# Routing attention and a bilinear FFN on one core: the second head pair's q and k loaded and transposed among the first pair's steps, and the first values ahead of the second scores

## The chip, the core and the metric

One core of a Trainium2 chip runs one program. Its engines are TensorE (PE; its weight loads are listed as PEld), VectorE (DVE), ScalarE (ACT), GpSimd (POOL) and SyncE (SP), which here issues most DMAs. The metric is the device time of one execution in microseconds. The kernel before took 1065.71 us as the median of four runs (1064.76, 1065.71, 1065.71 and 1065.93).

## The reference

Four batches of eight heads, 768 positions, head dimension 64. Every q and k row is assigned to the most similar of 16 centroids of its head; a query attends only to keys with its own assignment. The result, as 3072 tokens of 512 values, goes through a bilinear FFN of inner width 1536.

```python
q_assign = np.argmax(np.einsum('bhsd,hcd->bhsc', q_n, c_n), axis=-1)
k_assign = np.argmax(np.einsum('bhsd,hcd->bhsc', k_n, c_n), axis=-1)
mask = q_assign[:, :, :, None] == k_assign[:, :, None, :]
scores = scale * np.matmul(q, k.transpose(0, 1, 3, 2))
scores = np.where(mask, scores, -1000000000.0)
...
attn = attn / (np.sum(attn, axis=-1, keepdims=True) + 1e-09)
return np.matmul(attn, v).astype(np.float32)
...
a = x @ w_a
b = x @ w_b
return (a * b @ w_out).astype(np.float32)
```

## The kernel before, in words

The work goes by pairs of heads: 16 pairs p (4 batches of 4). A pair has 12 units: 2 halves of its 768 queries times 6 blocks of 128 keys. A unit's scores for both heads are one PSUM tile of 128 keys x 2 x 384 queries. Two units make a group g; a pair is six groups, so the main loop has 96 steps and three more to finish. The order of all instructions on each engine is the order in which the program issues them: nothing is rescheduled.

For each pair, q and k are loaded with positions on the partitions (`load`, L193 to L210, one DMA for each of q, k and head, 192 KB in pieces of 256 B, issued by SP) and transposed by PE, twelve blocks of 128 x 128 in three PSUM tiles (`prep_transpose(p, i)`, L335 to L350, one copy out of PSUM for each i). From these come the similarities to the centroids (`prep_sim`, L358, and its copy L366), turned back by PE (`prep_across`, L372), five DVE operations that make one-hot assignments (`prep_assign`, L405 to L409), and PE transposes of these (L418; for the first pair `prep_onehot_first`, L434, with a copy on ACT, L438, and one on DVE, L441).

`score` (L539) adds two products in PSUM, one of the one-hots (scaled by 2**60, bf16) and one of q and k, so that pairs of different assignment fall far below the others; then ACT takes the exponential (L548) into a tile `pt`, of which there are four. `weigh` multiplies these by v (L580). `add_up` (L569, DVE, later POOL too) sums the exponentials over the key blocks into `acc`, and `denominators` (L603) sums `acc` over the partitions by a product with ones. Only three PSUM tiles named m and two for scores (s) exist; one more (O) collects the values.

Pools set when things may start. The tile `qk` for loaded q and k exists once. The first pair takes another way in (`load_first`, L212 to L221): two DMAs bring its q (on SP's queue) and k (on ACT's) into a tile `h`, a buffer meant for the FFN's inner values, of which there are two, and DVE and ACT reorder them into `qk` (L224). `load(1)` then waits for the first pair's transposes, since it needs `qk` again.

The start is written out by hand before the loop: `keep_busy(n)` (L328) issues n transposes of the identity into a PSUM tile that nobody reads, while PE waits for other engines. In the loop, step g issues the scores of group g, the additions and the values of group g - 1, one of six preparation steps for the next pair (`prep_steps`), the rounding of the FFN weights as they fall due (`round_w`, L275 to L297: four DVE operations, one on ACT, one on POOL, then one more on DVE), and FFN pieces as far as credit goes. For the second pair, preparation step 0 issues `prep_transpose(1, 0)` and `(1, 1)`; the last third, `(1, 2)`, and `load(2)` follow at the end of the same step.

Of the kernel before, what the change touches and what calls it, by code (L numbers as in the profile page):

```python
# [8 lines left out]
FP32 = mybir.dt.float32  # L9
# [21 lines left out]
P = 128  # L31
# [105 lines left out]
def short_path(nc, tc, ctx, c, cn, centroids_in, casts, n_far, q, k, v,  # L137
# [3 lines left out]
    B, H, S, D = q.shape  # L141
    NC = 16
    DM, DF = moe_w_a.shape
    NJ = S // P
# [6 lines left out]
    def pool(name, bufs, space=None):  # L151
        kw = {} if space is None else {"space": space}
        return ctx.enter_context(tc.tile_pool(name=name, bufs=bufs, **kw))

    zero = pool("zero", 1)
    qkp = pool("qkp", 1)
# [8 lines left out]
    hp_ = pool("hp", 2)  # L165
# [9 lines left out]
    ident, identb, ones, rank = c["ident"], c["identb"], c["ones"], c["rank"]  # L175
# [10 lines left out]
    def by_blocks(p):  # L186
        return p >= HP

    def load(p):
        if p >= NPAIR:  # L190
            return
        b, hp = divmod(p, HP)
        if by_blocks(p):  # L193
            t = qkp.tile([P, 2, S // 32, 32], FP32, name="qk")
            for w, src in enumerate((q, k)):
                for n in range(4):
                    a, d = divmod(n, 2)
                    nc.sync.dma_start(
                        out=t[32 * n:32 * n + 32, w],
                        in_=src[b, 2 * hp + a, :, 32 * d:32 * d + 32].rearrange(  # L200
                            "(j t) d -> t j d", t=32))
            qks[p] = t
            return
        t = qkp.tile([P, 2, NJ, 2, D], FP32, name="qk")
        for w, src in enumerate((q, k)):
            for a in range(2):
                nc.sync.dma_start(
                    out=t[:, w, :, a, :],
                    in_=src[b, 2 * hp + a].rearrange("(p j) d -> p j d", j=NJ))
        qks[p] = t  # L210

    def load_first():  # L212

        t = qkp.tile([P, 2, NJ, 2, D], FP32, name="qk")
        rows = hp_.tile([P, 2, 2, NJ * D], FP32, name="h")
        for eng, w, src in ((nc.sync, 0, q), (nc.scalar, 1, k)):
            eng.dma_start(out=rows[:, w], in_=src[0, 0:2].rearrange(
                "a (p j) d -> p a (j d)", j=NJ))
        qks[0] = t
        return t, rows  # L220
# [20 lines left out]
            in_=v[b, 2 * hp:2 * hp + 2].rearrange("a (p j) d -> p a (j d)", j=NJ))  # L241

    first = load_first()
    centroids_in()
    order_first(*first, 0, nc.vector.tensor_copy)
    order_first(*first, 1, nc.scalar.copy)
# [76 lines left out]
    idle = ps_o.tile([P, 512], FP32, name="O")  # L323

    def keep_busy(n):

        for _ in range(n):
            nc.tensor.transpose(out=idle[:, 0:P], in_=ident, identity=ident)  # L328
# [7 lines left out]
    def prep_transpose(p, i):  # L336
        if i == 0:
            qkTs[p] = qtp.tile([P, 2 * S], FP32, name="qkT")
        ps = ps_m.tile([P, 512], FP32, name="m")
        for n in range(4):  # L340
            w, j = divmod(4 * i + n, NJ)
            nc.tensor.transpose(  # L342
                out=ps[:, n * P:(n + 1) * P],
                in_=qks[p][:, w, j].rearrange("p a d -> p (a d)"),
                identity=ident)
        dst = qkTs[p][:, i * 512:(i + 1) * 512]
        if p == 0 and i != 1:
            nc.vector.tensor_copy(out=dst, in_=ps)
        else:
            nc.scalar.copy(out=dst, in_=ps)  # L350
# [77 lines left out]
    def prep_onehot_first(kq):  # L428

        ohTs[0] = ohT_bufs[0]  # L430
        ps = ps_m.tile([P, 1024], BF16, name="m")
        for n in (3, 4, 5, 0, 1, 2):
            w, t = divmod(n, 3)
            nc.tensor.transpose(out=ps[:, n * P:(n + 1) * P],  # L434
                                in_=oh_all[:, 4 * t + 2 * w + kq, :],
                                identity=identb)
        c0 = kq * HB
        nc.scalar.activation(out=ohTs[0][:, S + c0:S + c0 + HB],  # L438
                             in_=ps[:, HB:S], func=AF.Identity, scale=FAR,
                             bias=nfar[:, 0:1])  # L440
        nc.vector.tensor_copy(out=ohTs[0][:, c0:c0 + HB], in_=ps[:, 0:HB])  # L441
# [55 lines left out]
    def prep_steps(p):  # L497
        if p >= NPAIR:
            return [lambda: None] * 6

        def both(*fs):
            return lambda: [f() for f in fs]

        if by_blocks(p):
            steps = prep_by_blocks(p)
            ready = [lambda s=s: todo.extend(s) for s in steps]
            ready[1] = both(lambda: prep_sim(p), lambda: load_v(p), ready[1])
            return ready

        return [  # L510
            both(lambda: prep_transpose(p, 0), lambda: prep_transpose(p, 1)),
            both(lambda: prep_sim(p), lambda: load_v(p)),
            lambda: todo.extend(prep_assign(prep_across(p))),
            lambda: None,
            lambda: prep_onehot(p, 1),
            lambda: None,
        ]
# [56 lines left out]
    def weigh(us):  # L574
        for u in us:
            p, hf, j = where(u)
            if j == 0:
                O_of[0] = ps_o.tile([P, 512], FP32, name="O")
            for a in range(2):
                nc.tensor.matmul(out=O_of[0][a * D:(a + 1) * D, 0:HB],  # L580
                                 lhsT=vs[p][:, a, j, :], rhs=probs[u][:, a, :],
                                 start=(j == 0), stop=(j == NJ - 1))
        if j < NJ - 1:
            return
        b, hp = divmod(p, HP)
        if hp == 0 and hf == 0:
            while b > 1 and len(ffn) > FREE_XT:
                ffn.popleft()[1]()
            xTs[b] = xtp.tile([P, NCH, S], FP32, name="xT")
        nc.scalar.copy(out=xTs[b][:, hp, hf * HB:(hf + 1) * HB],  # L590
                       in_=O_of[0][:, 0:HB])
# [403 lines left out]
    NG = NPAIR * GPP  # L995
# [13 lines left out]
    for i in range(8, len(w_parts)):  # L1009
        due.setdefault(23 + int((i - 8) / 1.5), []).append(i)  # L1010

    keep_busy(18)
    prep_transpose(0, 0)
    centroids_across()
    prep_transpose(0, 1)
    prep_transpose(0, 2)
    casts()
    for r, factor in ((slice(0, P // 2), 1.0), (slice(P // 2, P), FAR)):
        nc.vector.tensor_scalar(out=rank_far[r], in0=rank[r], scalar1=factor,
                                scalar2=None, op0=ALU.mult)  # L1020
    load(1)
    load_v(0)
    load_w(0)
    load_w(1)
# [3 lines left out]

    across = prep_across(0)
    rest_of_first = score((0, 1))  # L1030
    keep_busy(4)
    for kq in range(2):
        for step in prep_assign(across, kq):
            step()
        prep_onehot_first(kq)
        if kq == 0:
            keep_busy(5)
            rest_of_first()
            keep_busy(7)
    for g in range(NG + 3):  # L1040
        p, l = divmod(g, GPP)
        if l == 0:
            ready = prep_steps(p + 1)
        now = (2 * g, 2 * g + 1)
        before = (2 * g - 2, 2 * g - 1)
        if 0 < g < NG:
            score(now)
        check_inverses()
        if 0 < g <= NG:
            for u in before:  # L1050
                add_up(u)
        flush_w()
        if 0 < g <= NG:
            weigh(before)
        if g < NG:
            ready[l]()
        late = int(g > EARLY)
        if g % 3 == late and 0 < g - late:
            denominators(*divmod(g // 3 - 1, 2))
        parts = due.get(g, [])  # L1060

        def round_next():
            if parts:
                i = parts.pop(0)
                round_w(i)
                load_w(i + 2)

        round_next()
        if g <= EARLY:
            first, second = 4, 1  # L1070
        else:
            first, second = 5, 3 if g < NG else 2
        ph = {first: (p, 0), second: (p - 1, 1)}.get(l)
        halved = ph in den_of
        if halved:
            todo.extend(normalize(*ph))
        if ffn:
            credit += PER_GROUP[(g > 2 * BG + 3) + (g > 3 * BG + 3)]
            least = FREE_ROOM if halved and ph[1] and (ph[0] + 1) % HP == 0 else 0
            while len(ffn) > least and credit > 0:  # L1080
                cost, piece = ffn.popleft()
                credit -= cost
                piece()
                if todo:
                    todo.popleft()()
                round_next()
        else:
            credit = 0
        round_next()
        while todo:  # L1090
            todo.popleft()()
        if halved:
            ffn_ready(*ph)
        if l == 0 and p + 1 < NPAIR:
            if not by_blocks(p + 1):
                prep_transpose(p + 1, 2)
            load(p + 2)
        if l == 4 and p + 1 < NPAIR and not by_blocks(p + 1):
            prep_onehot(p + 1, 0)

    def some_ffn(n):
        for _ in range(n):
# [17 lines left out]
                     start=True, stop=True)  # L1120
# [227 lines left out]
```

## Time and profile before

| what | value |
|---|---|
| median of four runs | 1065.71 us |
| time of the profiled execution | 1064.65 us |
| its span | 1062.9 us, 13065 instructions |
| granted TensorE clock, mean | 0.999 |
| DVE, ACT, POOL busy | 67%, 24%, 33% of the span |
| DMA | 46.18 MB, 43 GB/s on average |
| q of the first pair, issue to landing | 3.9 us |
| k of the first pair, issue to landing | 4.4 us |

The span is measured inside the profiled execution, whose time is 1.75 us longer. The profile lists the busy time of each engine, groups of instructions by source line, the chain of work that ended last, and the instructions in order of time. A line of that last view gives start and duration in microseconds, the engine, the source line, the operation with what it writes and reads, and a count where equal instructions follow one another; in brackets stands the time that the engine had been idle and whose end it waited for. The ends of matmuls are modelled, so the starts are the better guide.

### The profile page before, as it was taken

The page shows a single profiled execution, that of the slowest core. Times are in us where ns is not written, and L with a number is a line of the kernel's source. Part 1 is how long each engine was busy: PE and PEld are TensorE (multiplying, and loading weights), DVE is VectorE, ACT ScalarE, POOL GpSimd, SP SyncE. Part 2 cuts the span into 40 slices and gives each one's busy share as a digit, 9 for nine tenths or more (in the row PEclk, how much of TensorE's full clock was granted, in tenths as well). Part 3 has the DMA queues.
Part 4 walks back from the last instruction along what each step waited for, and adds up shares of the span by engine and source line. Part 5 has one row for each costly group of instructions (what it writes and reads, how often), then busy time and mean ns, then how long its engine had stood idle before and what let it go on. Part 6 is the DMA issues. An engine that isn't in the chain of part 4 may idle for free.

```text
span 1062.9 us, 13065 instructions
## 1 busy us (share of the span) xinstructions
PE 1049.5 (99%) x4756; PEld 605.5 (57%) x4756; DVE 708.0 (67%) x1402; ACT 260.0 (24%) x501; POOL 354.3 (33%) x329
## 2 busy tenths in 40 slices
PE   8999999999999999999999999999999999999997
PEld 5444455554556665455445766555545687555686
DVE  5778877887857447676757736767565846676762
ACT  5665333233322221212222121122122200000000
POOL 1111345454533323443545422444334310222200
PEclk9999999999999999999999999999999999999999
DMA  5334243525130120202020030300000000000001
GB/s 169 94 72 99 84 105 104 124 74 134 62 47 16 41 43 20 39 4 45 4 45 1 25 65 24 46 0 20 0 4 1 11 30 21 0 1 1 0 31 33
DMA packets 120504, 46.18 MB, mean 43 GB/s; under 512 B 106608, under 2 KB 115824, under 8 KB 120432
## 3 DMA queue, kind: packets, MB, share of 16 engines
q1 hardware_dynamic: 120016, 44.85, 18.3%
q8 instruction: 39, 0.64, 0.2%
q10 hardware_dynamic: 416, 0.43, 0.1%
q14 instruction: 33, 0.27, 0.1%
HBM read 37.78 MB, written 6.29 MB: 41 GB/s over the span
## 4 chain that ended last, share of the span: by engine, by line
PE 92%; DVE 5%; issue 1%; POOL 1%; DMA 0%; ACT 0%; DVEq 0%; POOLq 0%
PE m L767 30%; PE m L893 20%; PE s L539 14%; PE O L580 12%; PE m L663 11%; PE m L603 2%; PE m L358 1%; DVE raw L723 1%; PE m L342 0%; DVE raw L750 0%; DVE acc L569 0%; DVE xT L723 0%; POOL xT L635 0%; DVE ha L777 0%; DMA wo_sb<-in_centroids_dram 0%
## 5 line engine op out<-in xcount | busy, mean ns | idle before, releaser
L548 ACT ACTIVATE pt<-s 128x768 f32<-128x768 f32 x192 | 145.4, 808 | 307.4 <-PE s L539 253.8
L569 POOL TENSOR_TENSOR acc<-acc,pt 128x384 f32<-128x384 f32 x144 | 151.9, 1068 | 59.8 <-ACT pt L548 43.6
L782 POOL TENSOR_TENSOR h<-h,ha 128x384 f32<-128x384 f32 x72 | 72.6, 1016 | 235.9 <-DVE ha L777 234.4
L580 PE MATMUL O<-pt,v 128*64 128x384 f32 x768 | 145.1, 499 | 0.0
L539 PE MATMUL s<-qkT 64*128 64x384 f32 x768 | 139.6, 482 | 0.0
L777 DVE TENSOR_TENSOR ha<-ha,m 128x384 f32<-128x384 f32 x126 | 66.9, 546 | 74.1 <-PE m L767 73.3
L777 DVE TENSOR_TENSOR h<-h,m 128x384 f32<-128x384 f32 x126 | 67.3, 549 | 64.3 <-PE m L767 63.5
L569 DVE TENSOR_TENSOR acc<-acc,pt 128x384 f32<-128x384 f32 x96 | 73.7, 793 | 35.9 <-POOL acc L569 35.0
L580 PEld LDWEIGHTS O<-pt,v 128*64 128x64 f32 x768 | 46.6, 136 | 86.4 <-issue 84.8
L539 PEld LDWEIGHTS s<-qkT 64*128 64x128 f32 x768 | 70.5, 187 | 31.4 <-issue 0.2
L893 PE MATMUL m<-wo_sb,h 128*128 128x256 f32 x384 | 87.5, 382 | 0.0
L635 POOL TENSOR_TENSOR xT<-xT,acc 128x384 f32<-128x384 f32 x32 | 32.9, 1029 | 147.9 <-DVE acc L630 121.3
L893 PEld LDWEIGHTS m<-wo_sb,h 128*128 128x128 f32 x384 | 72.1, 190 | 16.0 <-issue 4.2
L767 PE MATMUL m<-raw 128*128 128x384 f32 x192 | 70.4, 489 | 0.9 <-DVE ha L777 0.9
L663 PE MATMUL m<-xT,wa_sb 128*128 128x384 f32 x192 | 67.4, 493 | 0.7 <-POOL xT L635 0.7
L663 PE MATMUL m<-xT,wb_sb 128*128 128x384 f32 x192 | 66.8, 491 | 0.0
L893 PE MATMUL m<-xT,h 128*128 128x256 f32 x288 | 65.4, 382 | 0.1
L893 PEld LDWEIGHTS m<-xT,h 128*128 128x128 f32 x288 | 54.1, 190 | 11.7 <-issue 1.7
L767 PE MATMUL m<-xT,wa_sb 128*128 128x384 f32 x144 | 52.9, 491 | 0.4 <-DVE rest L899 0.4
L767 PE MATMUL m<-xT,wb_sb 128*128 128x384 f32 x144 | 52.9, 490 | 0.0
L767 PE MATMUL m<-xT,size 128*128 128x384 f32 x144 | 52.9, 490 | 0.0
L663 PEld LDWEIGHTS m<-xT,wa_sb 128*128 128x128 f32 x192 | 35.4, 190 | 30.5 <-ACT pt L548 3.6
(164 smaller groups left out, 1444.6 us busy)
## 6 DMA issues: line engine op xcount, KB each, us to landing
raw<-in_moe_w_a_dram SPq DMA_DIRECT2D x12, 512.0 KB, 4.3
raw<-in_moe_w_b_dram SPq DMA_DIRECT2D x12, 512.0 KB, 3.5
raw<-in_moe_w_out_dram SPq DMA_DIRECT2D x12, 512.0 KB, 3.2
qk<-in_q_dram SPq DMA_DIRECT2D x48, 96.0 KB, 2.9
qk<-in_k_dram SPq DMA_DIRECT2D x48, 96.0 KB, 3.6
v<-in_v_dram SPq DMA_DIRECT2D x24, 192.0 KB, 3.9
out_dram<-rest SPq DMA_DIRECT2D x24, 128.0 KB, 1.7
v<-in_v_dram SPq DMA_DIRECT2D x4, 384.0 KB, 4.6
```

The costliest lines, as they stand in the source:

```text
L358: nc.tensor.matmul(out=ps[32 * kq:32 * kq + 32, 0:HB], lhsT=cTb[:, hp, :], rhs=qkTs[p][:, kq * HB:(kq + 1) * HB], start=True, stop=True)
L539: nc.tensor.matmul(out=s[:, a, 0:HB], lhsT=Ts[p][r, S + j * P:S + (j + 1) * P], rhs=Ts[p][r, hf * HB:(hf + 1) * HB], start=start, stop=not ...
L548: nc.scalar.activation(out=pt, in_=s[:, :, 0:HB], func=AF.Exp, scale=SCALE)
L569: eng.tensor_tensor(out=acc[:, a, :], in0=probs[u - 1][:, a, :] if j == 1 else acc[:, a, :], in1=probs[u][:, a, :], op=ALU.add)
L580: nc.tensor.matmul(out=O_of[0][a * D:(a + 1) * D, 0:HB], lhsT=vs[p][:, a, j, :], rhs=probs[u][:, a, :], start=(j == 0), stop=(j == NJ - 1))
L603: nc.tensor.matmul(out=ps[a * D:(a + 1) * D, 0:HB], lhsT=ones, rhs=t[:, a, :], start=(n == 0), stop=(n == len(terms) - 1))
L635: nc.gpsimd.tensor_tensor(out=x, in0=x, in1=den, op=ALU.mult)
L663: nc.tensor.matmul(out=ps[:, 0:HB], lhsT=w_sb[:, ch, f * P:(f + 1) * P], rhs=xTs[b][:, ch, t0:t0 + HB], start=(ch == 0), stop=(ch == NCH - 1))
L767: nc.tensor.matmul(out=ps[:, 0:HB], lhsT=A[l][c], rhs=rhs[c], start=(c == 0), stop=(c == 1))
L777: nc.vector.tensor_tensor(out=out, in0=in0, in1=ps, op=op)
L782: nc.gpsimd.tensor_tensor(out=to, in0=to, in1=box[name], op=ALU.mult)
L893: nc.tensor.matmul(out=ps[:, 0:HN], lhsT=A[l][f // 3][:, f % 3, :], rhs=B[r][f // 2][:, f % 2, :], start=(f == 0), stop=(f == N2 - 1))
```

## The change

`load(1)` no longer uses `qk` but the second `h` tile, and moves to the very start, right behind the loads of the first pair; so its four DMAs come second on SP's queue, and the loads of v, of the first weights and of the third pair no longer stand behind them. The second pair's three `prep_transpose` calls leave loop step 0: the first takes the place of three fillers after the first scores, the other two that of the seven fillers after the first pair's one-hot product, in front of the second half of its one-hot transposes. The third copy out of PSUM goes to DVE instead of ACT. The first 18 fillers become twelve products of the tile `ones` (64 x 64) and 16 fillers. In loop step 1 the values of group 0 are issued ahead of the scores of group 1; in all later steps the order is as before.

```diff
-        t = qkp.tile([P, 2, NJ, 2, D], FP32, name="qk")
+
+        own, name = (hp_, "h") if p == 1 else (qkp, "qk")
+        t = own.tile([P, 2, NJ, 2, D], FP32, name=name)
...
     first = load_first()
+    load(1)
     centroids_in()
...
-        if p == 0 and i != 1:
+        if p == 0 and i != 1 or p == 1 and i == 2:
             nc.vector.tensor_copy(out=dst, in_=ps)
...
-            both(lambda: prep_transpose(p, 0), lambda: prep_transpose(p, 1)),
+            lambda: p > 1 and (prep_transpose(p, 0), prep_transpose(p, 1)),
...
-    keep_busy(18)
+    for _ in range(12):
+        nc.tensor.matmul(out=idle[0:D, 0:D], lhsT=ones, rhs=ones, start=True,
+                         stop=True)
+    keep_busy(16)
     prep_transpose(0, 0)
...
-    load(1)
     load_v(0)
...
     rest_of_first = score((0, 1))
-    keep_busy(4)
+    prep_transpose(1, 0)
+    keep_busy(1)
     for kq in range(2):
         for step in prep_assign(across, kq):
             step()
+        if kq == 1:
+            prep_transpose(1, 1)
+            prep_transpose(1, 2)
         prep_onehot_first(kq)
         if kq == 0:
             keep_busy(5)
             rest_of_first()
-            keep_busy(7)
     for g in range(NG + 3):
...
+        if g == 1:
+            weigh(before)
         if 0 < g < NG:
             score(now)
...
-        if 0 < g <= NG:
+        if 1 < g <= NG:
             weigh(before)
...
-            if not by_blocks(p + 1):
+            if p and not by_blocks(p + 1):
                 prep_transpose(p + 1, 2)
             load(p + 2)
```

## Prediction

> **What bounds the kernel now.** I read the engine table first, then the shares of the chain that ended last, then the first 31 us in order of time, because the change touches nothing after its loop's first step but the shift it hands on.
>
> ```profile
> PE 1049.5 (99%) x4756; PEld 605.5 (57%) x4756; DVE 708.0 (67%) x1402; ACT 260.0 (24%) x501; POOL 354.3 (33%) x329
> ...
> PE 92%; DVE 5%; issue 1%; POOL 1%; DMA 0%; ACT 0%; DVEq 0%; POOLq 0%
> ```
>
> PE is the bound: busy 99% and 92% of the chain. In the waits, all of PE's recorded idle time after 19 us sums to about 3 us. So a microsecond taken from PE's work before 19 us reaches the end, unless another engine takes it back on the way. The timeline of the start shows what can be taken (start, duration in us, engine, line, operation; in brackets the idle time before it and what ended it):
>
> ```profile
> 0.80 0.45 SPq L217 DMA_DIRECT2D h<-in_q_dram  x1
> 1.26 0.45 ACTq L217 DMA_DIRECT2D h<-in_k_dram  x1
> 1.43 4.10 PE L328 MATMUL O<-ident 128*128 128x128 f32 x18 [1.43 <-POOL ident masks.py:199]
> 5.83 0.91 ACT L224 COPY qk<-h 128x384 f32<-128x384 f32 x2
> 6.49 0.66 PE L342 MATMUL m<-ident,qk 128*128 128x128 f32 x4 [0.96 <-DVE nfar L302]
> ...
> 12.76 0.66 PE L328 MATMUL O<-ident 128*128 128x128 f32 x4
> 13.50 0.51 PE L434 MATMUL m<-identb,oh 128*128 128x128 bf16 x6
> 15.44 1.51 ACT L548 ACTIVATE pt<-s 128x768 f32<-128x768 f32 x2 [0.82 <-PE s L539]
> 15.50 0.99 PE L328 MATMUL O<-ident 128*128 128x128 f32 x7
> 16.91 0.51 PE L434 MATMUL m<-identb,oh 128*128 128x128 bf16 x6 [0.42 <-DVE oh L409]
> 17.25 1.04 PE L342 MATMUL m<-ident,qk 128*128 128x128 f32 x8
> 18.48 0.66 PE L342 MATMUL m<-ident,qk 128*128 128x128 f32 x4 [0.18 <-DVE ohT L441]
> 19.07 0.50 PE L539 MATMUL s<-ohT 64*128 64x384 bf16 x4
> 20.26 1.51 ACT L548 ACTIVATE pt<-s 128x768 f32<-128x768 f32 x2 [0.50 <-PE s L539]
> 20.79 1.51 PE L580 MATMUL O<-pt,v 128*64 128x384 f32 x8
> 24.50 0.68 DVE L297 SCALAR_TENSOR_TENSOR wa_sb<-size,wa_sb 128x512 f32<-128x512 f32 x1
> 26.75 0.56 DVE L405 TENSOR_REDUCE mx<-m 128x24 f32<-128x384 f32 x1 [1.57 <-PE m L372]
> 29.60 1.02 DVE L569 TENSOR_TENSOR acc<-acc,pt 128x384 f32<-128x384 f32 x2
> 30.20 0.29 PEld L603 LDWEIGHTS m<-acc,ones 128*64 128x64 f32 x2 [0.34 <-DVE acc L569]
> ```
>
> What to see: the L328 rows are filler while PE waits for VectorE (DVE): four at 12.76, seven at 15.50. The twelve transposes of the second pair (L342 at 17.25 and 18.48) are real work and hold PE from 17.25 until the second scores at 19.07: **1.82 us**, 0.35 of it a stall for a PSUM buffer. And at 30.20 PE already waits for DVE: DVE is the next limit close behind.
>
> **The change, part by part.**
>
> *Transposes into the gaps.* Four replace three of the four fillers at 12.76 (one stays): five instructions of 128 columns for four, 0.11 us more (the group of eight at 17.25: (1.04 - 0.27)/7 = 0.11 from start to start). They end by about 13.5, where PE waits for the one-hot of DVE anyway. Cost 0, at most 0.1. Eight replace seven fillers at 15.50: 8 x 0.11 = 0.9, next start about 16.4, and DVE ends its one-hot at 16.85. Cost 0. Removed from the path: the 1.82 us.
>
> *Their copies.* The first (ScalarE, ACT, 0.58) falls into ACT's wait before L438 at 14.04 and may push it by 0.03. The second (ACT, 0.58) stands in front of the second L438: 16.95 + 0.6, so L438 runs 17.6 to 18.2 instead of 17.45 to 18.03. The third (DVE, 0.69) runs 16.9 to 17.6, while L441 waits for L438 anyway. So DVE's chain of accumulations starts **0.15 us later** (L441 ends at 18.58 instead of 18.43).
>
> *First values ahead of the second scores.* PE's order becomes L434, values, scores, similarity. The values (8 instructions, 20.79 to 22.23: 1.44) can start at 17.25, since their exponentials end at 16.95 and v, now queued behind the second q and k, has some 6 us in hand. They end at 18.69, after L438 (18.2), so the scores do not wait: 18.69, before 19.07. Then scores 1.72 (19.07 to 20.79), so similarity at 20.41 instead of 22.23, and the third scores ready to start at 21.2 instead of 23.01: **1.8 us ahead**. The cover that goes: the values no longer stand between the second scores and the third, which reuse the second's PSUM. The exponentials start 1.19 after their scores (20.26 - 19.07), so they end at 19.88 + 1.51 = 21.4. The third scores' first half (0.17) needs only the first exponential, its second half meets 21.4 at 21.37. Cost 0.05; if the scores started 0.5 late it would be hidden too, since both shift.
>
> *DVE takes some back.* DVE's order is the same but for the one copy. Its row L297 ended at 25.18, then it idled 1.57 us until PE's L372 let it start L405 at 26.75. Now L372 comes 1.8 earlier, at about 24.95, but DVE is busy until 25.18 + 0.15 = 25.33. So L405 starts at 25.3: 1.45 us ahead, not 1.8. The five L405 to L409 operations and the accumulation at 29.60 follow without a gap, so at L603 PE, 1.8 ahead, waits for DVE, 1.45 ahead: its wait of 0.34 grows to about 0.7. After that both are 1.45 ahead, and from 41 us DVE has idle stretches of 2.1 us again. Sum: **-1.45 us**.
>
> *Warm-up.* 18 fillers become 12 small products on a tile ready at 1.03 and 16 fillers. The 18 run at (5.10 - 1.43)/17 = 0.216 us from start to start, twice the 0.11 seen from 6.49 on: the clock came up in between, though the column of granted clock reads 1.00 throughout. A product of 64 columns costs between 0.11 (half a 128-column filler) and 0.43 (two passes, each like a whole one); I take 0.22, two passes of half the columns, as products of this type show two rows in the trace. 12 x 0.22 = 2.6 from 1.05 to 3.65, then 16 fillers end at 7.1 if all are slow, 6.3 if the fast ones begin at 5.5. The first real transpose starts at 6.49. Cost 0 to 0.6, taken as 0.
>
> *The earlier load.* Four loads of 192 KB join SyncE's queue at 1.25, behind q, while k is in flight in ACT's. q lands at 0.80 + 3.9 = 4.7 and is used at 5.81; k lands at 1.26 + 4.4 = 5.66 (times to landing of the DMA table). Its copies end 1.0 us after landing; the last transposes of the first pair start at 7.93 after waiting for a PSUM buffer, and two of k's blocks (0.22) precede them. So k may land until 6.7: **1.0 us of slack**. If the new load halves what k gets after q has landed, 0.96 becomes 1.9 and k lands at 6.6. Cost 0. By 10 to 12 us the same load moved 185 and 176 GB/s alone, 1.1 us for each of four, so its data is there by about 9.5 and needed at 12.76. If k had to stand behind all four, it would land 4.4 late and cost 3.4. I take 0, since the only row with two queues at once (q and k) shows them sharing, 0.96 apart.
>
> [...]
>
> **Sum.** -1.82 (transposes) + 0.05 (PSUM) + 0.3 (DVE) = -1.45. The profiled execution took 1064.65 (span 1062.9), so 1063.2 against it; the median of the four runs is 1065.71, 1.06 above it, so **1064.3**.
>
> **Rivals.**
> 1. *k late.* The second pair's loads go ahead of k and delay it past its slack of 1.0 us. For: the DMA share is 1.0 in 3.0 to 4.0 us, nothing is to spare. Against: k's queue is its own. All four ahead: 3.4 - 1.45 = +1.9, so 1067.6. It decides from a k 2.45 us late, two loads and a bit.
> 2. *An earlier clock.* Three of the runs shown are about 1.0 above the fourth (1064.76) and the profile. If the clock came up after 6.49 in those, the transposes and similarities run at 0.216 for 0.11: 0.43 for the first four, as much for the last, some 1 us in all. PE busy from 1.05 without a pause would then remove it: 1064.76 - 1.45 = 1063.3. For: the 0.96 us gap of PE at 5.5. Against: no row of a late clock.
> 3. *Gain eaten.* The warm-up overruns by 0.6, or k by as much, and the exponentials of the second scores hold the third: half the gain or less, 1065.2. For: ACT takes the sim copy and a size operation ahead of the next exponentials. This is also the case in which the change does not do what it says, with the transposes waiting in their gaps.
>
> **How the numbers follow.** Forecast (1.2 to 1.8 gained, 1063.9 to 1064.5) 0.55; earlier clock 0.25; gain eaten 0.13; k late 0.07. 0.2% is 2.13 us, about what a measurement of this kernel can tell from no change: faster than 1063.58 is most of the earlier clock and a little of the forecast, 0.28; slower than 1067.84 only the worst of the late k, 0.05; within, 0.67. Range 1062.8 to 1066.0: from the earlier clock's 1063.3 less the scatter of 0.5, past the gain eaten; the late k is left out.
>
> **What would show it.** L580 ahead of the second scores at about 17.3; the third scores at 21.2 to 21.3; L405 of the second pair (26.75) at 25.3 with no wait on L372; the wait of PE for the accumulation at L603 grown to 0.6 or 0.7; k's copy on ACT before 6.7. Wrong if L342 starts after 6.6, if its transposes are 0.21 apart, or if PE at 40 us is not 1.3 to 1.6 ahead.

## The result, and the profile after

The changed kernel takes **1063.20 us** (median of 37 runs, 1062.81 to 1063.87); the kernel before, now with 57 runs, 1064.83 (1064.37 to 1065.95). The ratio is 0.9983, with a 95% interval of 0.9978 to 0.9987: 0.17% faster. The profiled execution took 1063.32 with a span of 1061.5, 1.33 and 1.4 below those of before. The prediction said 1064.3, within 1062.8 to 1066.0, and 1063.2 against the profiled execution.

The two sets of runs have different shapes. Those of before fall into two groups, 34 from 1064.37 to 1065.03 (mean 1064.67) and 23 from 1065.34 to 1065.95 (mean 1065.67), with nothing between. Those of the changed kernel form one group (mean 1063.25). So 1.42 of the change of the mean, 1.82, is the distance from the lower group, to which the profiled execution of before (1064.65) belongs, and the other 0.40 (23/57 of 1.0) is the share of the upper group in the mean of before. This is arithmetic on the runs of before; what the path and the new warm-up each bring is measured below.

The page of the changed kernel: its busy times and the shares of the chain are those of before to within one percentage point, PE still the bound.

```profile
PE 1049.7 (99%) x4768; PEld 606.0 (57%) x4768; DVE 708.5 (67%) x1403; ACT 259.7 (24%) x500; POOL 354.6 (33%) x329
...
PE 93%; DVE 4%; issue 1%; POOL 1%; DMA 0%; ACT 0%; DVEq 0%; POOLq 0%
```

Its timeline, for the rows that answer to those shown of before. Line numbers grow by two or three: L345 is the transposes, L437 the one-hot transposes, L583 the values, L542 the scores, L441 ACT's one-hot copy, L300 the last rounding operation, L408 the first assignment operation, L375 the similarities turned back, L606 the product with ones.

```profile
1.08 2.82 PE L1016 MATMUL O<-ones 128*64 128x64 f32 x24 [1.08 <-DVE ones L80]
3.83 2.81 PE L331 MATMUL O<-ident 128*128 128x128 f32 x16
3.98 0.23 DVE L94 TENSOR_TENSOR wo_sb<-wo_sb 128x64 f32<-128x64 f32 x1 [2.95 <-DMA wo_sb<-in_centroids_dram]
6.77 0.66 PE L345 MATMUL m<-ident,qk 128*128 128x128 f32 x4
...
13.04 0.66 PE L345 MATMUL m<-ident,h 128*128 128x128 f32 x4
15.78 1.09 PE L345 MATMUL m<-ident,h 128*128 128x128 f32 x8
17.18 0.51 PE L437 MATMUL m<-identb,oh 128*128 128x128 bf16 x6 [0.31 <-DVE oh L412]
17.62 1.51 PE L583 MATMUL O<-pt,v 128*64 128x384 f32 x8
17.73 0.58 ACT L441 ACTIVATE ohT<-m,nfar 128x384 bf16<-128x384 bf16 x1
19.07 0.50 PE L542 MATMUL s<-ohT 64*128 64x384 bf16 x4
...
21.57 0.59 PE L542 MATMUL s<-ohT 64*128 64x384 bf16 x4
24.77 0.68 DVE L300 SCALAR_TENSOR_TENSOR wa_sb<-size,wa_sb 128x512 f32<-128x512 f32 x1
24.82 0.55 PE L375 MATMUL m<-ident,sim 128*128 128x128 f32 x3
...
25.41 0.56 DVE L408 TENSOR_REDUCE mx<-m 128x24 f32<-128x384 f32 x1
...
28.37 0.81 PE L606 MATMUL m<-pt,ones 128*64 128x384 f32 x4
28.86 0.29 PEld L606 LDWEIGHTS m<-acc,ones 128*64 128x64 f32 x2 [0.35 <-DVE acc L572]
```

Two rows of before belong beside these, the third scores and the first product with ones:

```profile
23.01 0.50 PE L539 MATMUL s<-ohT 64*128 64x384 bf16 x4
...
29.71 0.81 PE L603 MATMUL m<-pt,ones 128*64 128x384 f32 x4
```

What to see: from 1.08 to its first real work at 6.77 PE has no listed wait (0.96 before); the second pair's transposes stand at 13.04 and 15.78, and at 17.18 PE still waits 0.31 for DVE, so they cost nothing: 17.18 is 10.41 after the first transposes (6.77), and 16.91 before was 10.42 after them (6.49). The values follow at 17.62, the second scores at 19.07, the same time as before, but the values are already behind them; the third scores come at 21.57 instead of 23.01. L408 has no wait in front of it any more (1.57 before). The wait at L606 is what it was, 0.35. All of this although the start was 0.28 late: L94, which waits for the centroids, starts at 3.98 instead of 3.70, and L345 at 6.77 instead of 6.49. Because starts differ so, positions are compared below from equal starts, that is, counted from the first pair's first transposes in the same trace.

### The profile page after: what moved, and what is told of

It is laid out like the page before. It is cut to its first block, busy times and chain, and to the rows that moved or that the text cites. A ratio compares the mean times of both kernels' runs of the same rounds, so it can differ in the third digit from the quotient of the medians.

```text
span 1061.5 us, 13089 instructions
## 1 busy us (share of the span) xinstructions
PE 1049.7 (99%) x4768; PEld 606.0 (57%) x4768; DVE 708.5 (67%) x1403; ACT 259.7 (24%) x500; POOL 354.6 (33%) x329
## 4 chain that ended last, share of the span: by engine, by line
PE 93%; DVE 4%; issue 1%; POOL 1%; DMA 0%; ACT 0%; DVEq 0%; POOLq 0%
PE m L770 30%; PE m L896 20%; PE s L542 15%; PE O L583 12%; PE m L666 12%; PE m L606 2%; PE m L361 1%; DVE raw L726 1%; PE m L345 0%; DVE raw L753 0%; POOL xT L638 0%; DVE xT L726 0%; DMA wo_sb<-in_centroids_dram 0%; DVE ha L780 0%; DVE acc L572 0%
## 5 line engine op out<-in xcount | busy, mean ns | idle before, releaser
L583 PE MATMUL O<-pt,v 128*64 128x384 f32 x768 | 145.1, 499 | 0.0
L542 PE MATMUL s<-qkT 64*128 64x384 f32 x768 | 139.7, 482 | 0.0
L583 PEld LDWEIGHTS O<-pt,v 128*64 128x64 f32 x768 | 46.6, 136 | 86.0 <-issue 84.3
L542 PEld LDWEIGHTS s<-qkT 64*128 64x128 f32 x768 | 70.5, 187 | 31.3 <-issue 0.2
```

Of the source, the lines that this page charges most:

```text
L542: nc.tensor.matmul(out=s[:, a, 0:HB], lhsT=Ts[p][r, S + j * P:S + (j + 1) * P], rhs=Ts[p][r, hf * HB:(hf + 1) * HB], start=start, stop=not ...
L583: nc.tensor.matmul(out=O_of[0][a * D:(a + 1) * D, 0:HB], lhsT=vs[p][:, a, j, :], rhs=probs[u][:, a, :], start=(j == 0), stop=(j == NJ - 1))
```

## The experiments

Three things were open: which part brings the 1.4, and whether DVE or PE is the limit behind it; whether the early load delayed the centroids; and what the upper group of runs was. Each kernel ran eleven times beside the kernel before.

**The order of the values alone, and the transposes alone.** First the changed kernel without the new order:

```diff
-        if g == 1:
-            weigh(before)
...
-        if 1 < g <= NG:
+        if 0 < g <= NG:
             weigh(before)
```

> The changed kernel with the old order in loop step 1: the second scores ahead of the first values. Theory: the scores must wait for ACT's second one-hot copy (L441, ends 0.7 us after PE is free) with nothing to do behind them, so the gain of the moved transposes falls by 0.5: the third scores 0.5 later than in the changed kernel, time about 1063.7. Rival: the order does not matter, since PE has the same work either way; 1063.2.

Measured 1063.46 (1063.20 to 1063.89). The timeline shows the stall:

```profile
17.41 0.34 PE L542 MATMUL s<-ohT 64*128 64x384 bf16 x2
...
18.15 0.34 PE L542 MATMUL s<-ohT 64*128 64x384 bf16 x2 [0.41 <-ACT ohT L441]
18.32 1.45 PE L542 MATMUL s<-qkT 64*128 64x384 f32 x8
...
21.93 0.50 PE L542 MATMUL s<-ohT 64*128 64x384 bf16 x4
...
28.63 0.81 PE L606 MATMUL m<-pt,ones 128*64 128x384 f32 x4
```

Two products run, two wait for ACT. Its third scores stand at 21.93, 15.36 after its L345 (6.57); in the changed kernel 14.80 after (21.57 - 6.77). So 0.56 is lost there and 0.46 is still lost at the product with ones (28.63, 22.06 after, against 28.37, 21.60 after). The medians differ by 0.26 only, but they come from different sets of runs. Against the lower group of the kernel before in its own set the mean is 0.99 lower here (1063.48 against 1064.47) and 1.42 lower for the changed kernel: a difference of 0.43, close to the trace's 0.46. Then the opposite, the kernel before with the same two lines moved to the new order:

> The kernel before with only the new order in loop step 1: the values of group 0 ahead of the scores of group 1, all transposes where they were. Theory: PE's work between its wait at 18.5 and the third scores is the same, so no gain; the third scores wait 0.1 for the exponentials of the second. Time as before or 0.1 above, two groups of runs as before. Rival: the order itself brings the gain, then 0.5 or more below.

Measured 1064.66 (1064.30 to 1065.75), against 1064.63 beside it, in two groups. Its third scores run 0.59 instead of 0.50: a wait of 0.09 for the exponentials. So the order alone is worth nothing; it is worth 0.46 once PE has no other work for the wait. The transposes bring 1.16 (the product with ones came 29.71 - 6.49 = 23.22 after the first transposes before, 22.06 without the new order), the order 0.46.

**Is DVE the next limit?** Both kernels with 0.9 us more work on DVE ahead of L300:

```diff
-        nc.vector.tensor_scalar(out=wi, in0=hi, scalar1=3, scalar2=0x3FFFFFF8,
-                                op0=ALU.logical_shift_left,
-                                op1=ALU.bitwise_and)
+        for _ in range(3 if i == 0 else 1):
+            nc.vector.tensor_scalar(out=wi, in0=hi, scalar1=3, scalar2=0x3FFFFFF8,
+                                    op0=ALU.logical_shift_left,
+                                    op1=ALU.bitwise_and)
```

> The changed kernel with 0.9 us more work on DVE: the first operation of the first weight's rounding (L278, 0.42 us) runs three times instead of once, with the same outcome. Theory: in the changed kernel DVE ends its weight work (L300) just when PE's similarities come (L375), so all 0.9 go to the accumulation that PE waits for at L606; the time rises by 0.8 to 0.9, to about 1064.1. Rival: PE alone is the bound there and DVE has slack left; no change.

> The kernel before with the same 0.9 us more on DVE. Theory: DVE idles 1.57 us there before L405, so this costs nothing: 1064.6 and the second group at 1065.7, and the idle time falls to 0.7. Rival: DVE's work costs the same wherever it stands, 0.8 more in both kernels; then the pair says nothing on slack.

Measured 1063.99 (1063.75 to 1064.40) for the changed kernel with the added work, 0.8 more than without; 1065.39 (1064.28 to 1065.62) for the one before, where four runs lie in the lower group (1064.28 to 1064.72) and seven in the upper (1065.31 to 1065.62), so no group has moved; only more runs than usual fell into the upper one. The changed kernel with more DVE work, at the product with ones:

```profile
29.60 0.19 PEld L607 LDWEIGHTS m<-acc,ones 128*64 128x64 f32 x2 [1.22 <-DVE acc L573]
```

and the kernel before with the same:

```profile
31.07 0.30 PEld L604 LDWEIGHTS m<-acc,ones 128*64 128x64 f32 x2 [0.34 <-DVE acc L570]
```

The wait of 0.35 grew to 1.22 in the one (by 0.87, what was added) and stayed at 0.34 in the other, where DVE's wait ahead of the first assignment operation fell from 1.57 to 0.67 instead. DVE had 1.57 us of slack before and has none after: in the changed kernel L300 ends at 24.77 + 0.68 = 25.45, the similarities (L375, 24.82, 0.55 long) at 25.37. They meet within 0.1. The change has used up exactly what DVE could hide.

**The early load and the centroids.** First the kernel before with nothing but the early load (the load's two edits in the diff of the change):

> The kernel before with only the early load of the second pair into the second h tile; its transposes stay where they were. Theory: the centroids land 0.28 later, L94 at 3.98, all the rest with it, the time rises by 0.28 (groups at about 1064.9 and 1066.0). Rival (scatter): no change, 1064.6 and 1065.7. If the early load also removes a wait of the transposes at 17.2, the time would fall; the trace of before shows no DMA wait there, so I expect none.

Measured 1064.75 (1064.31 to 1065.96), six runs in a lower group (1064.31 to 1064.75) and five in the upper: no 0.28. Its L94 starts at 3.61, earlier than in the kernel before. Then the changed kernel with the load held back; a small copy on POOL, which reads the squares of the centroids and writes into the tile to be loaded, makes the load wait:

```diff
     first = load_first()
-    load(1)
     centroids_in()
+    load(1)
...
         t = own.tile([P, 2, NJ, 2, D], FP32, name=name)
+        if p == 1:
+            for w in range(2):
+                nc.gpsimd.tensor_copy(out=t[:, w, 0, :, 0:1],
+                                      in_=wo_sb[:, 0, D:D + 2][:, :, None])
```

> The changed kernel, with the second pair's four loads held back until VectorE has squared the centroids (a small copy on POOL stands in between). Theory: in the changed kernel the centroids landed 3.2 us after issue and not 2.9, k 4.9 and not 4.4, because the four loads join the queue at once; that shifted everything by 0.28 us. Without it L94 starts at 3.7 again, L345 at 6.5, and the time falls by 0.28 to about 1062.9. Rival: the 0.28 is scatter of one execution; then the time stays at 1063.2 and landings differ from execution to execution whatever the load does. Second rival: the load now lands too late for the transposes at 12.8; then L345 of the second pair waits for a DMA and the time rises.

Measured 1062.96 (1062.74 to 1063.50). Its start is that of before to 0.01 us, so its rows compare directly with those of before:

```profile
3.70 0.23 DVE L94 TENSOR_TENSOR wo_sb<-wo_sb 128x64 f32<-128x64 f32 x1 [2.67 <-DMA wo_sb<-in_centroids_dram]
...
6.49 0.66 PE L349 MATMUL m<-ident,qk 128*128 128x128 f32 x4 [0.24 <-DVE nfar L309]
...
17.34 1.51 PE L587 MATMUL O<-pt,v 128*64 128x384 f32 x8
...
21.29 0.60 PE L546 MATMUL s<-ohT 64*128 64x384 bf16 x4
...
28.08 0.82 PE L610 MATMUL m<-pt,ones 128*64 128x384 f32 x4
```

From equal starts the product with ones comes at 28.08 instead of 29.71: **1.63 us** earlier. That is the gain of the path. Whether the load itself costs the changed kernel 0.2 was then asked on one chip, with the changed kernel beside it:

> The changed kernel itself, on the same chip as the two that follow, since 0.2 us is what is asked. So far it stood at 1063.2 in other jobs, the late load at 1062.96. Theory of scatter (centroids land anywhere between 2.7 and 3.2 us after issue whatever the kernel): all three kernels here have the same lower edge and the same median but for the second group of the old warm-up, within 0.1. Rival (the early load together with the new warm-up delays the centroids): this one is 0.2 above the late load, and its trace has L94 at 3.8 or later.

> The changed kernel with the second pair's loads held back until the centroids are squared, beside the changed kernel on one chip. Scatter: same median within 0.1. Rival: 0.2 below, L94 at 3.7.

Measured 1063.18 (1062.72 to 1063.49) for the changed kernel and 1062.92 (1062.66 to 1063.67) for the late load. Over all its runs the late load has a mean of 1063.02 (22 runs, standard deviation 0.28), the changed kernel 1063.23 (48 runs, 0.23): 0.2 apart, which the runs on one chip alone do not settle. The landings do not support the cause that I gave. L94 starts at 3.98 and 3.79 in the two traces of the changed kernel, 3.70 and 3.56 with the late load and 3.86 with the late load and 13 fillers, but 3.61 with the early load in the kernel before. Over the traces of all kernels it runs from 3.46 to 3.98, and with the old warm-up (3.46 to 3.75) it is no later with the early load than without. So a delay by the load alone falls. A delay by the early load and the new warm-up together does not: the four traces with both have L94 at 3.78 to 3.98 and land k 4.7 to 4.9 us after issue, the four with the new warm-up and no early load at 3.56 to 3.86 and 4.3 to 4.6. The traces are few and the ranges of L94 overlap, so whether the 0.2 comes from there stays open.

**The upper group of runs.** The changed kernel with the old 18 fillers, twice, and the kernel before with the new warm-up:

```diff
-    for _ in range(12):
-        nc.tensor.matmul(out=idle[0:D, 0:D], lhsT=ones, rhs=ones, start=True,
-                         stop=True)
-    keep_busy(16)
+    keep_busy(18)
```

> The changed kernel with the 18 fillers of before at the start. The runs of before fall into two groups, one around 1064.6 and one around 1065.7; those of the changed kernel lie in one, around 1063.2. Theory: the new warm-up has removed the upper group (a later clock). Then this kernel shows two groups again, about 1063.2 and 1064.3, and PE idles from 5.5 to 6.8. Rival: the upper group came from the fillers and transposes after 12 us, or from the order of loads; then this kernel stays in one group at 1063.2.

> The changed kernel with the 18 old fillers, beside the changed kernel on one chip. Both theories: runs of a late clock between 1063.6 and 1064.2, which the other two lack. Scatter: its lower runs at the changed kernel's median. Rival: its lower runs 0.2 below, at the late load's.

> The kernel before with only the new warm-up (twelve small products and 16 fillers). Theory: one group of runs around 1064.6, none around 1065.7, so the median falls by 0.2 to 1.0 with no step on the path changed. Rival (the groups have nothing to do with the warm-up): two groups as before, median about 1064.8.

With the old fillers the runs spread again: seven from 1062.89 to 1063.23 and four from 1063.67 to 1064.18 in the first set, six from 1062.64 to 1063.19 and five from 1063.78 to 1064.38 in the second. The kernel before with the new warm-up has nine of eleven runs from 1064.17 to 1064.79 and two at 1065.00 and 1065.23; the upper group of the runs beside it starts at 1065.52. The profiled execution of the first set took 1063.69, so it belongs to the upper runs, and its timeline shows their cause:

```profile
1.43 4.10 PE L331 MATMUL O<-ident 128*128 128x128 f32 x18 [1.43 <-POOL ident masks.py:199]
6.40 1.11 PE L345 MATMUL m<-ident,qk 128*128 128x128 f32 x4 [0.87 <-DVE nfar L305]
...
7.52 1.91 PE L345 MATMUL m<-ident,qk 128*128 128x128 f32 x8
```

The first pair's transposes, 1.11 for four and 1.91 for eight, where the trace of before has 0.66 for four: they run at the spacing of the first fillers, 0.216 us, twice the 0.11 of the trace of before. I read this as a clock that had not come up; the column of granted clock reads 1.00 here too, and only the durations tell. The spacing does not halve at the same time in all traces: at about 4.3 us in that of the kernel without the new order (my estimate from its 16 fillers, 2.13 us long from 3.83 on), after 9.2 in this one. Of six traces with the 18 fillers, three have the spacing 0.11 from the first transpose on (at 6.49 in the kernel before) and three have 0.216 until after 9.2. Those with 0.216 are executions of 1063.69 and 1063.92 (the changed kernel with the old fillers) and 1065.39 (the kernel before with more DVE work), those with 0.11 of 1064.31, 1064.55 and 1064.65 (the kernel before, alone or with the early load or the new order): the former stand in the upper group of their kernels, the latter in the lower.

These sets also separate the path from the warm-up. With the old fillers in both kernels, the changed one is 1.51 and 1.58 lower in the lower group (means 1063.01 against 1064.52, 1062.96 against 1064.53) and 1.75 and 1.43 in the upper one: about the path's 1.63. The new warm-up lowers the mean by 0.2 to 0.3 (the kernel before from 1064.98 to 1064.67; the changed kernel from 1063.44 to 1063.16 on one chip, 0.17 over all its runs), but the medians hardly at all (1064.65 to 1064.62; 1063.19 to 1063.18). Which of its differences does this, the start 0.35 us earlier, products in place of the first transposes, or filler that lasts until the real work, no run separates.

The new warm-up does not do away with the late clock, it changes its price. In the trace of the changed kernel that ran beside the late load (1063.49) all 16 fillers ran slow:

```profile
3.83 3.51 PE L331 MATMUL O<-ident 128*128 128x128 f32 x16
7.18 0.60 PE L345 MATMUL m<-ident,qk 128*128 128x128 f32 x4
```

They end at 7.34, the transposes behind them run fast, and the fillers have held back these transposes by about 0.6: they could have started at 6.6 (L94 at 3.79, and 2.79 from L94 to L345). The 16 fillers took 2.13 to 2.81 us in the six other traces, and there they held back the transposes by 0.03 at most. So I tried 13 of them with the late load:

> The late load with 13 fillers in place of 16 at the start. Theory: in executions with a late clock the 16 fillers, at 0.216 us each from 3.84, end at 7.3 and hold the first transposes, ready at 6.4 to 6.8, by up to 0.7; thirteen end at 6.65 at the slow clock and 5.7 or so at the fast one. So the upper edge of the runs falls from 1063.5 to 1063.3 or less, the median to about 1062.8. Rival: fewer fillers leave PE idle before 6.5, the clock comes later and the first transposes run at 0.216 apart; then runs near 1064 appear, as with the old warm-up.

Measured 1062.93 (1062.67 to 1063.32), ratio to before 0.9982 (0.9972 to 0.9991). No run near 1064, and the upper edge is 0.2 to 0.35 lower than in the two sets with 16; the median is that of the late load and did not fall. The fillers of its trace run 3.85 to 6.47, mostly slow, and its first transposes start at 6.64 without delay. This and the late load with 16 are the lowest of all kernels here, 0.2 below the changed one, which is about as much as these runs can tell.

## Why the prediction was right, point by point

The time lay in the range and the path's mechanism was as forecast, but 1064.3 itself was 1.1 too high, and part of the agreement is luck (see the earlier clock, below).

- **The transposes in the gaps cost nothing, 1.82 leaves the path.** Right. PE waits 0.31 for DVE after all twelve.
- **Values at 17.25, done before ACT's one-hot copy matters.** Right but for 0.10: they start 0.44 after the one-hot transposes (17.62 - 17.18), not 0.34.
- **PSUM wait of the third scores, 0.05.** Right in kind, 0.09 measured (0.59 for 0.50; likewise with the order alone).
- **ACT's extra copy pushes L438, and DVE starts its accumulation 0.15 late.** Wrong. I added 0.6 to the end of the exponentials; but the copy (L353) started at 17.12, 0.12 before the listed end of the exponentials (15.73 + 1.51 = 17.24), and ended at 17.71, when PE's one-hot transposes ended too (17.18 + 0.51 = 17.69). L441 starts 0.55 after L437 (17.73 - 17.18) where L438 started 0.54 after L434. The mis-sized term is 0.15; it is 0.
- **DVE takes 0.3 back, the wait at L603 grows to 0.7.** Wrong in size, right in place. Without the 0.15 DVE and PE meet at L408 within 0.1, and the wait stays at 0.35. The pair of kernels with more DVE work shows that DVE is the limit from that point: of the added work, 0.87 was paid in the changed kernel and nothing in the one before.
- **Sum -1.45.** From equal starts it was -1.82 + 0.10 + 0.09 = -1.63, as measured. Against the profiled execution, where I had set it, 1.33 came out, because its centroids landed 0.28 later; I had no term for that, and L94 scatters by 0.5 over the traces (3.46 to 3.98).
- **The sign of being wrong, L342 after 6.6.** It came true, at 6.77, though the forecast held: the fillers ended at 6.64, and what made it late were the centroids. The sign could not tell an overrun from a late load. The sign at 40 us held: the scores at 38.56 came at 37.22, 1.34 ahead.
- **The early load is free; k has 1.0 us of slack.** Right for k. It landed 4.9 us after issue instead of 4.4 in the changed kernel, 4.5 with the early load alone, half of the slack at most; the last transposes of the first pair come 1.44 after its first in both traces (8.21 - 6.77, 7.93 - 6.49). The rival of a late k had no part. Whether the early load costs 0.2 in another way is open, as said above.
- **The earlier clock.** As a cause it was priced rightly at 1.0 and it exists, but it isn't why 1064.3 missed 1063.20 by 1.1: with the old fillers, where the late clock stays, the medians were 1063.09 and 1063.19. The miss comes from the 1.06 that I added for the median of four runs. Three of those four lay in the upper group, where only 23 of 57 do; the median of the 57 is 1064.83, and 1064.83 - 1.45 = 1063.4. The four times showed it: one at 1064.76 and three at 1065.71 to 1065.93, with the profiled execution at 1064.65, are two groups, and a median of them belongs to one. The forecast against the profiled execution, 1064.65 - 1.45 = 1063.2, needed no such choice. That the range took in 1063.20 is partly luck: its lower end came from the rival of the earlier clock, which by itself moves the mean by 0.2 to 0.3 and the median hardly at all. Its 1063.3 (1064.76 - 1.45) took for granted that a PE busy without a pause has its clock up earlier, and no run shows that: in the trace of 1063.49 PE has no listed wait between 1.08 and its first transposes at 7.18, and all 16 fillers ran at 0.216. What the runs show is that the changed kernel, with the new warm-up as a whole, has no upper group in 37 runs.
- **Overrun of the warm-up, 0 to 0.6, taken as 0.** Both ends occur: 0.6 in one trace with 16 fillers, 0.03 at most in the six others.

## What to carry to other kernels

Work moved into a wait is worth what it took on the path only until the next engine is met, so measure the slack of that engine at the next meeting point first (here the 1.57 us in front of L405, of which the 1.63 gained left nothing). An order of two steps that costs nothing while other work fills a wait can become a cost once that work is moved away, so look at it again. And look at the single times before taking their median: where they fall into two groups, a median of a few belongs to one of them by chance, and a forecast built on it is off by the distance between the groups.

## What the runs showed of the hardware that was not expected

The spacing of equal 128-column fp32 transposes at the start, which I read as PE's clock, was 0.216 us at first and 0.11 later, and the time at which it halved differed between executions of one kernel: the 16 fillers of the changed kernel took 2.81 us in one trace and 3.51 in another. Over the traces this time lies between about 4.3 us (an estimate, three fillers into the trace of the kernel without the new order) and after 9.2 us (the changed kernel with the old fillers). The profile's clock column reads 1.00 in all slices of the trace of before from 1.5 to 20 us and of that of the changed kernel from 1.5 to 15. Halving late costs 1.0 us with the old warm-up (1065.67 against 1064.67) and about 0.6 in the one trace with the new one in which all fillers ran slow. Loads of the first microsecond land with a scatter of their own: the centroids 2.6 to 3.2 us after issue, over fourteen traces of kernels that issue them alike.
